# One start for every transfer: moving the data of every other SBUF slot by 128 bytes

## Chip, cores and metric

The kernel runs on one core of a Trainium2 chip. Its time is device time in microseconds, from one launch. Before the change three runs gave 1687.97, 1688.45 and 1688.55 us; their median is 1688.45 us.

The engines go by short names: PE (TensorE, matrix products and transposes), DVE (VectorE), ACT (ScalarE), POOL (GpSimd) and SP (SyncE, which here does nothing but issue transfers). HBM is the memory off the core, SBUF the one on it, with 128 partitions; PSUM takes what PE computes.

## What is computed

One decoding step of an attention block with a cache, followed by a gated feed-forward block, forwards and backwards. The results are the output and the gradients of eight inputs.

```python
def _A_ref(x, k_cache, v_cache, wq, wo):        # x: 4 x 1 x 512
    q = (x @ wq).reshape(B, 1, 32, 128).transpose(0, 2, 1, 3)
    scores = einsum("bhqd,bhkd->bhqk", q, k_cache) * (128 ** -0.5)
    p = softmax(scores)
    o = einsum("bhqk,bhkd->bhqd", p, v_cache)   # caches: 4 x 32 x 4096 x 128, bf16
    return o.transpose(0, 2, 1, 3).reshape(B, 1, 4096) @ wo
...
h = x + _A_ref(layernorm(x), k_cache, v_cache, wq, wo)
return h + swiglu(layernorm(h), w1, w3, w2)     # 512 -> 1792 -> 512
...
out, vjp = jax.vjp(f, x, k_cache, v_cache, wq, wo, w1, w3, w2)
return (out, *vjp(grad_out))
```

There are 4 x 32 = 128 heads. For each, K and V are 4096 x 128 in bf16, 1 MB. The gradients of the two caches, `out_2` and `out_3`, have the same size. So K is read once, V twice (forwards and backwards), and both gradients are written once: five times 134 MB, beside which the weights and their gradients are small.

## The kernel before

**The arena.** Nearly all SBUF data lives in one tile, `arena` (L112), of 23 slots. A slot is `SLOT` = 4160 elements of bf16 in each partition, 8,320 bytes. One head of K or V takes 4096 of them (32 rows of 128 in each partition), 8,192 bytes. The 4160 come from the tile `PK`, in which each of the 32 rows has two columns more (`PKW` = 130). In the built program the arena begins at byte 30,336 of each partition.

`Slot` (L125) takes one slot from the list `free` and makes a view of it, `self.t`; `b`, `f` and `heads` are views of that as bf16, as fp32 and as 32 rows of 128. `Slot2` (L146) takes two neighbouring slots that begin at an even number and views them as one piece, for two heads at once. `give` returns slots to the list. Which slot is taken depends on what was given back when, and not on addresses.

**The order of the work** is written out by hand (`tc.manual_schedule()`): each engine does its instructions in the order of the program text. All large transfers are issued by SP, on one queue; a transfer into a slot waits until the slot's last reader or writer is done.

**Forward** (L650 to L712): 64 groups of two heads. K and V of each head are loaded into slots (`load_K` L175, `load_V` L182; 1 MB each). K is transposed, a quarter by PE through PSUM (`T_pe` L352, copied back by ACT) and three quarters by DVE (`T_dve` L361). The scores (`S_head` L375) give the softmax; DVE multiplies K by the probabilities into a `PK` slot (`PK_mul` L455), PE multiplies V by that (`M_mm` L466), and ACT puts the 128 x 129 result of each head into an `M` slot (`M_end` L474, 16 heads in a slot, fp32). `PK` and `M` need more than 8,192 bytes of their slot.

**Middle** (L714 to L969): the output projection, the feed-forward block and the start of its backward pass. The weights are transposed here.

**Backward** (from L972): the first 32 heads one by one, the other 96 as 48 pairs of heads. V is loaded a second time (`load_V2` L836, 1 MB; `load_pair` L1292, 2 MB) and transposed in place by PE and ACT (`words_T` L793). The gradients of V and K are outer products that DVE writes into fresh slots (`outer` L812, `outer_pair` L1399), and SP stores them (`grad_V` L820, `grad_K` L1267, `grad_pair` L1407; 1 MB and 2 MB). The gradients of the weights go out in between (`side_work` L1017).

A transfer of a single head is 128 packets of 8,192 bytes, one for each partition, and one completion record on each of the 16 DMA engines. A pair of heads is 128 packets of 16,384 bytes.

Of the kernel before, what the change touches and what calls it, by code (L numbers as in the profile page):

```python
# [9 lines left out]
FP32 = mybir.dt.float32  # L10
# [7 lines left out]
SLOT = 4160  # L18
# [3 lines left out]
SP = 32  # L22
NPAIR = 8
OLD = 9


@with_exitstack
def kernel(
# [22 lines left out]
    nc = tc.nc  # L51
    P = nc.NUM_PARTITIONS

    B = A_x.shape[0]
    D = A_x.shape[-1]
    H = A_k_cache.shape[1]
    Sk = A_k_cache.shape[2]
    Dh = A_k_cache.shape[3]
    F = B_w1.shape[1]
    NH = B * H  # L60
# [4 lines left out]
    SJ = Sk // P  # L65
# [3 lines left out]
    PKW = Dh + 2  # L69
    MC = 16  # L70
# [41 lines left out]
    arena = slotp.tile([P, NSLOT * SLOT], BF16, name="arena")  # L112
# [12 lines left out]
    class Slot:  # L125
        def __init__(self, name, src=free):
            self.i = src[0]
            if part["B"] and src is free:
                lone = sorted((i for i in free if i not in part["pairs"]), key=age, reverse=True)
                self.i = lone[0] if name in SIDE or lone and age(lone[0]) >= OLD else max(free, key=age)  # L130
            src.remove(self.i)
            self.t = arena[:, self.i * SLOT:(self.i + 1) * SLOT]

        def b(self, n=4096):
            return self.t[:, 0:n]
# [10 lines left out]
    class Slot2:  # L146
# [5 lines left out]
        def __init__(self):  # L152
            self.i = min(self.choices())[1]
            free.remove(self.i)
            free.remove(self.i + 1)
            self.t = arena[:, self.i * SLOT:(self.i + 2) * SLOT]

        def give(self):
            gave(self.i, self.i + 1)
# [13 lines left out]
    Ks, Vs, KTs, PKs = {}, {}, {}, {}  # L173
# [34 lines left out]
    for i in range(2):  # L208
        t = fcon.tile([P, 64], BF16, name=f"onesw{i}")
# [4 lines left out]
    def ones_window(col):  # L214
# [11 lines left out]
                          in_=rowg[:, None, :, None].to_broadcast([P, 4, 8, 4]))  # L226
# [17 lines left out]
    OT_f = pers.tile([P, NH], FP32, name="OT_f")  # L244
# [80 lines left out]
    Ms = []  # L325

    def M_of(s):
        return Ms[s // MC].f(MC * (Dh + 1)).rearrange("p (n c) -> p n c", c=Dh + 1)[:, s % MC, :]

    c1 = ExitStack()  # L330
    c1b = ExitStack()
# [117 lines left out]

    def PK_pairs(s):  # L450
        PKs[s] = Slot("PK")
        PK = PKs[s].t[:].rearrange("p (j c) -> p j c", c=PKW)
        nc.gpsimd.tensor_copy(out=PK[:, :, Dh:PKW], in_=P_all[:, s, :, None].to_broadcast([P, SJ, 2]))  # L453

    def PK_mul(s):  # L455
        PK = PKs[s].t[:].rearrange("p (j c) -> p j c", c=PKW)
        nc.vector.tensor_tensor(  # L457
            out=PK[:, :, 0:Dh].rearrange("p j (r t) -> p j r t", t=2),
            in0=Ks[s].heads().rearrange("p j (r t) -> p j r t", t=2),
            in1=PK[:, :, None, Dh:PKW].to_broadcast([P, SJ, Dh // 2, 2]),  # L460
            op=ALU.mult,
        )
        Ks.pop(s).give()
        kdone["n"] += 1

    def M_mm(s, j0, j1):  # L466
        if j0 == 0:
            hold["M"] = psM.tile([P, PKW], FP32, name="M_ps", tag="M")
        PK = PKs[s].t[:].rearrange("p (j c) -> p j c", c=PKW)
        Vn = Vs[s].heads()  # L470
        for j in range(j0, j1):
            nc.tensor.matmul(hold["M"][:], lhsT=Vn[:, j, :], rhs=PK[:, j, :], start=(j == 0), stop=(j == SJ - 1))  # L472

    def M_end(s):  # L474
        w = s % 32
        PK = PKs[s].t[:].rearrange("p (j c) -> p j c", c=PKW)
        if w == 0:
            hold["kP"] = psK.tile([P, 4, Dh], FP32, name="kP_ps", tag="kP")
        for c in range(2):
            for q in range(4):  # L480
                j0 = (c * 4 + q) * 4
                nc.tensor.matmul(hold["kP"][32 * q:32 * (q + 1), :, :], lhsT=ones_window(w), rhs=PK[:, j0:j0 + 4, 0:Dh],  # L482
                                 start=(w == 0 and c == 0), stop=(w == 31 and c == 1), tile_position=(0, 32 * q))
        if s % MC == 0:
            Ms.append(Slot("M"))
        nc.scalar.copy(out=M_of(s), in_=hold["M"][:, 0:Dh + 1])
        PKs.pop(s).give()
        Vs.pop(s).give()
# [10 lines left out]


    def O_cols(s0, s1):
        nc.vector.tensor_copy(out=OT_f[:, s0:s1], in_=Ms[s0 // MC].f(MC * (Dh + 1)).rearrange("p (n c) -> p n c", c=Dh + 1)[
            :, s0 % MC:s0 % MC + s1 - s0, Dh])
        nc.vector.tensor_copy(out=OT_bf[:, s0:s1], in_=OT_f[:, s0:s1])

# [337 lines left out]
    with ExitStack() as cm:  # L843
# [70 lines left out]
        for sl in w1 + w3:  # L914
            sl.give()
        rs = Slot("reps")
# [1 line left out]
        part["pairs"] = {j for i in kept for j in (i, i + 1)}  # L918
        rep_bufs = {nm_: [rs.b()[:, (2 * k + i) * 512:(2 * k + i + 1) * 512].rearrange("p (i d) -> p i d", i=REP) for i in range(2)]
                    for k, nm_ in enumerate(("rq", "rdo"))}  # L920
        dh = rs.f(2080)[0:B, 1024:1024 + D]
        while len(free) > 1:
            load_V2()

# [47 lines left out]
    with ExitStack() as c2:  # L972
# [44 lines left out]
        def side_work():  # L1017
# [1 line left out]
            nc.tensor.transpose(pt[:], OT_bf[:], ident_b[:])  # L1019
            nc.scalar.copy(out=O_sb[:], in_=pt[:])  # L1020
            yield
            t = rs.f(2080)[:, 1536:1536 + NH]
            nc.vector.tensor_tensor(out=t, in0=c_rep[:], in1=kPT[:], op=ALU.mult)
            nc.vector.tensor_tensor(out=t, in0=dq_ps[:, 0:NH], in1=t, op=ALU.subtract)
            nc.vector.tensor_scalar(out=dqT_bf[:], in0=t, scalar1=scale, scalar2=None, op0=ALU.mult)
# [93 lines left out]
            for i in range(2):  # L1119
                st = Slot("gw2")  # L1120
                hw = hh_rows[:, i * 7 * P:(i + 1) * 7 * P].rearrange("b (p k) -> b k p", k=7)
                for k in range(7):
# [4 lines left out]
                                  in_=st.b(7 * D).rearrange("p (c j) -> p c j", c=7))  # L1127
# [4 lines left out]
            for (rows, out_ap) in ((dg_rows, out_6), (du_rows, out_7)):  # L1132
                for i in range(2):
                    st = Slot("gw13")
                    nw = hhat_bf[0:B, i * 2 * P:(i + 1) * 2 * P].rearrange("b (p k) -> b k p", k=2)
                    for k in range(2):
                        for (f0_, w_) in f_chunks:
# [5 lines left out]
                                      in_=st.b(2 * F).rearrange("p (c f) -> p c f", c=2))  # L1143
                    st.give()
            r1.give()
            for h0 in range(0, H, 8):
                st = Slot("gwo")
                ow = oflat.b(HD)[0:B, h0 * P:(h0 + 8) * P].rearrange("b (p k) -> b k p", k=8)
                for k in range(8):
# [4 lines left out]
                                  in_=st.b(8 * D).rearrange("p (k j) -> p k j", k=8))  # L1154
# [143 lines left out]
        def load_pairs(t):  # L1298
            while npv["next"] < NT and (npv["next"] <= t or len(V2s) + 2 * len(pV) < 6 and len(Slot2.choices()) > 1
                                          and -min(Slot2.choices())[0] >= OLD - 2):  # L1300
                load_pair()
# [197 lines left out]
        for t in range(NT):  # L1499
            s = SP + 2 * t  # L1500
# [46 lines left out]
```

## Time and profile before

The profiled execution spans 1686.6 us from its first to its last instruction, 1.8 us less than the median of the runs.

| | |
|---|---|
| median of 3 runs | 1688.45 us |
| span of the profiled execution | 1686.6 us |
| bytes moved | 707.21 MB (422.59 read from HBM, 282.34 written) |
| mean rate over the span | 419 GB/s |
| loads of K, forwards | 128 of 1024 KB, 15.4 us from issue to landing (median) |
| loads of V, single heads | 160 of 1024 KB, 15.6 us |
| loads of V, pairs | 48 of 2048 KB, 31.7 us |
| stores of gradients, single heads and weights | 72 of 1024 KB, 19.8 us |
| stores of gradients, pairs | 96 of 2048 KB, 27.4 us |

How to read it: a digit in a row of slices is the busy share of one fortieth of the span, in tenths. Busy shares of engines are averages over stages, so they say which engine can bound a stage and not that it does. A transfer's time from issue to landing contains its wait behind the transfers ahead of it on the same DMA engines: a single head's packets alone need about 2.5 us. Where the text speaks of a packet's duration, it is that of the trace's record of this packet; where it says where a transfer begins, the address comes from the built program.

### The profile page before, as it was taken

What the parts mean: (1) busy time and instruction counts of PE and PEld (TensorE: products, weight loads), DVE (VectorE), ACT (ScalarE), POOL (GpSimd) and SP (SyncE); (2) the same over time, 40 slices, a digit from 0 to 9 for tenths busy, and PEclk for the clock granted to TensorE, in tenths of its full rate; (3) what the DMA queues carried; (4) which work ended last, traced back from release to release, by engine and by line L of the source; (5) the groups of instructions that cost most, each with busy time, mean ns of one, the idle gap of its engine ahead of it and who ended that gap; (6) DMA issues with size and microseconds to landing.
All of it is one profiled execution on the core that took longest, in us unless ns stands there. A gap on an engine that the chain in (4) does not pass through costs nothing.

```text
span 1686.6 us, 33967 instructions
## 1 busy us (share of the span) xinstructions
PE 1260.6 (75%) x14188; PEld 924.3 (55%) x14188; DVE 1233.9 (73%) x1198; ACT 960.9 (57%) x1492; POOL 379.6 (23%) x663
## 2 busy tenths in 40 slices
PE   5989888888888888878878666667766677776660
PEld 4777777677667766745555544544434444444440
DVE  5999899989998997667766476576565656555673
ACT  3455454445445454677666556666655676666650
POOL 1221222222232222234541131111120101011020
PEclk9999999999999999799899778777678676567775
DMA  9999999999999999999999999999999999999996
GB/s 400 424 424 424 425 423 425 424 424 421 418 423 411 424 411 397 398 410 426 425 426 428 429 429 429 431 430 429 429 430 430 429 429 431 430 429 431 430 429 259
DMA packets 80986, 707.21 MB, mean 419 GB/s; under 512 B 8748, under 2 KB 12984, under 8 KB 15296
## 3 DMA queue, kind: packets, MB, share of 16 engines
q1 hardware_dynamic: 80416, 704.94, 99.2%
q8 instruction: 112, 1.84, 0.4%
q14 instruction: 42, 0.34, 0.0%
q0 software_dynamic: 416, 0.10, 0.0%
HBM read 422.59 MB, written 282.34 MB: 418 GB/s over the span
## 4 chain that ended last, share of the span: by engine, by line
DMA 35%; DVE 7%; ACT 5%; PE 5%; issue 3%; DVEq 0%; SPq 0%; POOL 0%; ACTq 0%
DMA out_dram<-arena 34%; DVE arena L1400 7%; ACT arena L799 5%; PE pt_tps L798 1%; PE dq_ps L1007 1%; PE dP_ps L1245 1%; DMA arena<-in_A_v_cache_dram 1%; PE pt_wo L610 0%; DVEq L1542 0%; PE rep_ps L1186 0%; DVE dPr L1342 0%; ACT dPr L1221 0%; PE dOT_ps L773 0%; PE dPT_ps L1228 0%; PE c_ps L784 0%
## 5 line engine op out<-in xcount | busy, mean ns | idle before, releaser
L799 ACT COPY arena<-pt_tps 128x1024 bf16<-128x1024 bf16 x512 | 491.7, 1023 | 249.0 <-PE pt_tps L798 247.3
L798 PE MATMUL pt_tps<-ident_f,arena 128*128 128x128 f32 x2048 | 410.7, 356 | 202.9 <-DMA arena<-in_A_v_cache_dram 125.6
L798 PEld LDWEIGHTS pt_tps<-ident_f,arena 128*128 128x128 f32 x2048 | 304.1, 182 | 349.3 <-issue 191.6
L1400 DVE TENSOR_TENSOR arena<-arena 128x8192 bf16<-128x8192 bf16 x48 | 212.5, 4427 | 197.9 <-DMA out_dram<-arena 192.5
L457 DVE TENSOR_TENSOR arena<-arena 128x4096 bf16<-128x4096 bf16 x128 | 292.4, 2285 | 24.0 <-POOL arena L453 24.0
L472 PE MATMUL M_ps<-arena 128*128 128x130 bf16 x4096 | 286.9, 223 | 30.0 <-DMA arena<-in_A_v_cache_dram 29.2
L472 PEld LDWEIGHTS <-arena 128*128 128x128 bf16 x4096 | 254.6, 99 | 49.6 <-DMA arena<-in_A_v_cache_dram 42.5
L1400 DVE TENSOR_TENSOR arena<-dS,arena 128x8192 bf16<-128x8192 bf16 x48 | 212.3, 4424 | 67.6 <-DMA out_dram<-arena 67.6
L364 DVE STREAM_TRANSPOSE arena<-arena 128x512 f32<-128x512 f32 (+1 forms) x321 | 250.6, 797 | 0.0
L359 ACT COPY arena<-pt_tps 128x1024 bf16<-128x1024 bf16 x128 | 129.4, 1012 | 180.4 <-PE pt_tps L358 149.6
L1397 POOL COPY arena<-arena 128x128 bf16<-128x128 bf16 x48 | 43.7, 912 | 432.7 <-ACT arena L1374 200.0
L370 POOL TENSOR_TENSOR W<-qrep,wmask 128x128 bf16<-128x128 bf16 x128 | 120.8, 944 | 85.4 <-PE S_ps L390 70.6
L453 POOL COPY arena<-P_all 128x64 bf16<-128x64 bf16 x128 | 32.7, 256 | 412.5 <-ACT P_all L447 409.5
L1308 POOL COPY arena<-arena 64x4 bf16<-64x4 bf16 x96 | 68.8, 717 | 136.3 <-PE dP_ps L1328 108.6
L1328 PE MATMUL dP_ps<-arena 128*32 128x512 bf16 x768 | 84.4, 471 | 8.4 <-ACT arena L799 8.3
L813 DVE TENSOR_TENSOR arena<-dS,arena 128x4096 bf16<-128x4096 bf16 x32 | 73.1, 2291 | 21.8 <-DMA out_dram<-arena 21.5
L447 ACT COPY P_all<-pt_P 32x64 bf16<-32x64 bf16 x256 | 52.1, 203 | 54.1 <-PE pt_P L443 51.8
L358 PE MATMUL pt_tps<-ident_b,arena 128*128 128x128 bf16 x1024 | 80.8, 224 | 0.0
L482 PE MATMUL kP_ps<-arena,onesw 128*32 128x512 bf16 x1024 | 79.4, 387 | 0.0
L813 DVE TENSOR_TENSOR arena<-P,arena 128x4096 bf16<-128x4096 bf16 x29 | 66.3, 2291 | 17.7 <-DMA out_dram<-arena 17.5
L422 ACT ACTIVATE E<-S_ps,nm 128x256 f32<-128x256 f32 x64 | 30.4, 474 | 82.7 <-DVE nm L419 82.6
L991 PE MATMUL gps<-arena 4*128 4x512 bf16 x110 | 47.3, 452 | 39.0 <-ACT arena L985 39.0
(246 smaller groups left out, 1494.7 us busy)
## 6 DMA issues: line engine op xcount, KB each, us to landing
out_dram<-arena SPq DMA_DIRECT2D x96, 2048.0 KB, 27.4
arena<-in_A_v_cache_dram SPq DMA_DIRECT2D x160, 1024.0 KB, 15.6
arena<-in_A_k_cache_dram SPq DMA_DIRECT2D x128, 1024.0 KB, 15.4
arena<-in_A_v_cache_dram SPq DMA_DIRECT2D x48, 2048.0 KB, 31.7
out_dram<-arena SPq DMA_DIRECT2D x72, 1024.0 KB, 19.8
arena<-in_A_wq_dram SPq DMA_DIRECT2D x8, 1024.0 KB, 14.3
arena<-in_B_w_dram SPq DMA_DIRECT2D x8, 896.0 KB, 15.0
out_dram<-arena SPq DMA_DIRECT2D x6, 896.0 KB, 27.6
```

The costliest lines, as they stand in the source:

```text
L358: nc.tensor.transpose(pt[:, i, :], Kn[:, c * GW + i, :], ident_b[:])
L359: nc.scalar.copy(out=KT[:, c * GW:(c + 1) * GW, :], in_=pt[:])
L364: nc.vector.transpose(out=KT[:, c * w_:(c + n) * w_], in_=Kn[:, c * w_:(c + n) * w_])
L370: nc.gpsimd.tensor_tensor(out=W[:, hl], in0=qrep[:, :, s:s + 1].to_broadcast([P, 4, 32]), in1=wmask[:, hl, None, :].to_broadcast([P, 4, 32 ...
L457: nc.vector.tensor_tensor(out=PK[:, :, 0:Dh].rearrange("p j (r t) -> p j r t", t=2), in0=Ks[s].heads().rearrange("p j (r t) -> p j r t", t=2),
L472: nc.tensor.matmul(hold["M"][:], lhsT=Vn[:, j, :], rhs=PK[:, j, :], start=(j == 0), stop=(j == SJ - 1))
L482: nc.tensor.matmul(hold["kP"][32 * q:32 * (q + 1), :, :], lhsT=ones_window(w), rhs=PK[:, j0:j0 + 4, 0:Dh], start=(w == 0 and c == 0), stop ...
L798: nc.tensor.transpose(ptw[:, jj, :], w[:, 4 * g + jj, :], ident_f[:])
L799: nc.scalar.copy(out=v.rearrange("p (j d) -> p j d", d=Dh)[:, g * GW:(g + 1) * GW, :], in_=pt[:])
L813: nc.vector.tensor_tensor(out=dst.rearrange("p j (r t) -> p j r t", t=2), in0=col2[:, :, None, :].to_broadcast([P, SJ, Dh // 2, 2]), in1=r ...
L1328: nc.tensor.matmul(rows["acc"][32 * c:32 * (c + 1), :], lhsT=zt[t % B][:, k, ZP - m:ZP - m + 32], rhs=words_of(v, 2 * c + u, k), start=(pl ...
L1400: nc.vector.tensor_tensor(out=dst.rearrange("p (j r t) -> p j r t", r=Dh // 2, t=2), in0=col2[:, :, None, :].to_broadcast([P, 2 * SJ, Dh / ...
```

## The change

Slots of even number, and pairs of slots, hold their data 64 elements (128 bytes) further on. `Slot` keeps the whole slot as `self.w`; its data view `self.t` has 4096 elements and begins at `LEAD` in even slots, at 0 in odd ones. `PK` and `M`, which need the whole slot and are part of no transfer, use `self.w`. A pair's view begins at `LEAD` and runs to the end of its second slot. Two views of the slot `rs` are taken from 2048 instead of 2080 fp32 elements, since `self.t` is shorter; the elements that they use are the same. No slot is chosen in another way, and the program text issues the same instructions in the same order.

```diff
--- before.py
+++ after.py
@@ -22,6 +22,7 @@
 SP = 32
 NPAIR = 8
 OLD = 9
+LEAD = 64
 
 
 @with_exitstack
@@ -129,7 +130,9 @@
                 lone = sorted((i for i in free if i not in part["pairs"]), key=age, reverse=True)
                 self.i = lone[0] if name in SIDE or lone and age(lone[0]) >= OLD else max(free, key=age)
             src.remove(self.i)
-            self.t = arena[:, self.i * SLOT:(self.i + 1) * SLOT]
+            self.w = arena[:, self.i * SLOT:(self.i + 1) * SLOT]
+            o = (self.i + 1) % 2 * LEAD
+            self.t = self.w[:, o:o + SJ * Dh]
 
         def b(self, n=4096):
             return self.t[:, 0:n]
@@ -153,7 +156,7 @@
             self.i = min(self.choices())[1]
             free.remove(self.i)
             free.remove(self.i + 1)
-            self.t = arena[:, self.i * SLOT:(self.i + 2) * SLOT]
+            self.t = arena[:, self.i * SLOT + LEAD:(self.i + 2) * SLOT]
 
         def give(self):
             gave(self.i, self.i + 1)
@@ -325,7 +328,7 @@
     Ms = []
 
     def M_of(s):
-        return Ms[s // MC].f(MC * (Dh + 1)).rearrange("p (n c) -> p n c", c=Dh + 1)[:, s % MC, :]
+        return Ms[s // MC].w[:].bitcast(FP32)[:, 0:MC * (Dh + 1)].rearrange("p (n c) -> p n c", c=Dh + 1)[:, s % MC, :]
 
     c1 = ExitStack()
     c1b = ExitStack()
@@ -449,11 +452,11 @@
 
     def PK_pairs(s):
         PKs[s] = Slot("PK")
-        PK = PKs[s].t[:].rearrange("p (j c) -> p j c", c=PKW)
+        PK = PKs[s].w[:].rearrange("p (j c) -> p j c", c=PKW)
         nc.gpsimd.tensor_copy(out=PK[:, :, Dh:PKW], in_=P_all[:, s, :, None].to_broadcast([P, SJ, 2]))
 
     def PK_mul(s):
-        PK = PKs[s].t[:].rearrange("p (j c) -> p j c", c=PKW)
+        PK = PKs[s].w[:].rearrange("p (j c) -> p j c", c=PKW)
         nc.vector.tensor_tensor(
             out=PK[:, :, 0:Dh].rearrange("p j (r t) -> p j r t", t=2),
             in0=Ks[s].heads().rearrange("p j (r t) -> p j r t", t=2),
@@ -466,14 +469,14 @@
     def M_mm(s, j0, j1):
         if j0 == 0:
             hold["M"] = psM.tile([P, PKW], FP32, name="M_ps", tag="M")
-        PK = PKs[s].t[:].rearrange("p (j c) -> p j c", c=PKW)
+        PK = PKs[s].w[:].rearrange("p (j c) -> p j c", c=PKW)
         Vn = Vs[s].heads()
         for j in range(j0, j1):
             nc.tensor.matmul(hold["M"][:], lhsT=Vn[:, j, :], rhs=PK[:, j, :], start=(j == 0), stop=(j == SJ - 1))
 
     def M_end(s):
         w = s % 32
-        PK = PKs[s].t[:].rearrange("p (j c) -> p j c", c=PKW)
+        PK = PKs[s].w[:].rearrange("p (j c) -> p j c", c=PKW)
         if w == 0:
             hold["kP"] = psK.tile([P, 4, Dh], FP32, name="kP_ps", tag="kP")
         for c in range(2):
@@ -499,7 +502,7 @@
 
 
     def O_cols(s0, s1):
-        nc.vector.tensor_copy(out=OT_f[:, s0:s1], in_=Ms[s0 // MC].f(MC * (Dh + 1)).rearrange("p (n c) -> p n c", c=Dh + 1)[
+        nc.vector.tensor_copy(out=OT_f[:, s0:s1], in_=Ms[s0 // MC].w[:].bitcast(FP32)[:, 0:MC * (Dh + 1)].rearrange("p (n c) -> p n c", c=Dh + 1)[
             :, s0 % MC:s0 % MC + s1 - s0, Dh])
         nc.vector.tensor_copy(out=OT_bf[:, s0:s1], in_=OT_f[:, s0:s1])
 
@@ -918,7 +921,7 @@
         part["pairs"] = {j for i in kept for j in (i, i + 1)}
         rep_bufs = {nm_: [rs.b()[:, (2 * k + i) * 512:(2 * k + i + 1) * 512].rearrange("p (i d) -> p i d", i=REP) for i in range(2)]
                     for k, nm_ in enumerate(("rq", "rdo"))}
-        dh = rs.f(2080)[0:B, 1024:1024 + D]
+        dh = rs.f(2048)[0:B, 1024:1024 + D]
         while len(free) > 1:
             load_V2()
 
@@ -1019,7 +1022,7 @@
             nc.tensor.transpose(pt[:], OT_bf[:], ident_b[:])
             nc.scalar.copy(out=O_sb[:], in_=pt[:])
             yield
-            t = rs.f(2080)[:, 1536:1536 + NH]
+            t = rs.f(2048)[:, 1536:1536 + NH]
             nc.vector.tensor_tensor(out=t, in0=c_rep[:], in1=kPT[:], op=ALU.mult)
             nc.vector.tensor_tensor(out=t, in0=dq_ps[:, 0:NH], in1=t, op=ALU.subtract)
             nc.vector.tensor_scalar(out=dqT_bf[:], in0=t, scalar1=scale, scalar2=None, op0=ALU.mult)
```

## The prediction

> **What bounds the kernel now.** I read the page's 40 slices first, then its queue line, then a table of stages, and last the costliest groups.
>
> ```profile
> span 1686.6 us, 33967 instructions
> ...
> PE 1260.6 (75%) x14188; PEld 924.3 (55%) x14188; DVE 1233.9 (73%) x1198; ACT 960.9 (57%) x1492; POOL 379.6 (23%) x663
> ...
> DMA  9999999999999999999999999999999999999996
> GB/s 400 424 424 424 425 423 425 424 424 421 418 423 411 424 411 397 398 410 426 425 426 428 429 429 429 431 430 429 429 430 430 429 429 431 430 429 431 430 429 259
> DMA packets 80986, 707.21 MB, mean 419 GB/s; under 512 B 8748, under 2 KB 12984, under 8 KB 15296
> ...
> q1 hardware_dynamic: 80416, 704.94, 99.2%
> ...
> DMA 35%; DVE 7%; ACT 5%; PE 5%; issue 3%; DVEq 0%; SPq 0%; POOL 0%; ACTq 0%
> ```
>
> No engine passes 75%, but the DMA row stands at 9 in every slice but the last, and SP's queue (q1) alone fills 99.2% of sixteen DMA engines' time. The chain of waits has DMA as its largest share, but follows only the last link at each step; the queue's own 99.2% is the better witness. So the time is the sum of the packets, and the change can act only through how long a packet takes or whether the queue runs dry.
>
> ```profile
> core 0: us, PE busy (x) PEld busy (x) DVE busy (x) ACT busy (x) POOL busy (x), PEclk, DMA share, GB/s
> ...
> 40.00:480.00 440.00, 380.33 (x6319) 311.74 (x6318) 406.59 (x542) 224.26 (x496) 110.44 (x264) 0.99 1.01 423
> ...
> 900.00:1620.00 720.00, 497.97 (x3100) 324.78 (x3100) 439.26 (x226) 463.17 (x573) 112.20 (x152) 0.74 1.01 430
> 1620.00:1687.00 67.00, 13.46 (x80) 8.24 (x79) 38.16 (x19) 11.77 (x13) 8.86 (x2) 0.60 0.75 319
> ```
>
> This is the table by stages; the last two columns are the share of the DMA engines' time and the rate. From 40 to 480 us only single heads are loaded; by the addresses worked out below, 53% of those bytes start 128 bytes off. From 900 to 1620 us nearly all is pairs of heads, and 98% of the bytes start off. The stage with nearly everything off moves more, 430 against 423 GB/s. Its packets are also twice as long, so this alone settles nothing, and I go to the packets.
>
> **The change, part by part.** The arena begins at byte 30,336 of each partition, which is 118.5 times 256; a slot is 8,320 bytes, 32.5 times 256. So an even slot, and every pair (it begins at an even slot), starts 128 bytes past a multiple of 256, an odd slot on one. Of SP's 530 transfers 361 start off (155 single loads of heads or wq/wo pages, 3 of weights, 48 pair loads, 53 single stores, 6 weight stores, 96 pair stores), 528 of 705 MB. Afterwards none does: even slots and pairs move up by LEAD, 64 elements or 128 bytes. The pattern does what its words say.
>
> 1. *Instructions, waits, queues.* The built programs have the same instructions with the same waits in the same order on all five engines. Nothing is added, removed or moved past anything: 0 us, and no cover is needed.
>
> 2. *A packet that starts off.* This is the whole question. The trace records each packet with size and duration. Of 47,104 packets of 8,192 bytes, 44,289 took 309 ns (94%); of 18,432 of 16,384 bytes, 17,428 took 611 ns (95%). The next packet of the same DMA engine begins 3 to 4 ns before the one ahead ends, so these durations are the throughput. A further 8,192 bytes cost 611 - 309 = 302 ns, so 128 bytes' worth of time is 302/64 = 4.72 ns. Single heads lie in both kinds of slot, so if starting off cost that, the 8,192-byte packets would fall into two groups of similar weight, 4.7 ns apart. There is one group.
>
> The same at the scale of a transfer: the 16 completion records of each transfer give a median time, and the difference to the transfer before is its interval. Behind another transfer of one slot, transfers of one slot that start on a multiple of 256 come 2,453 ns apart (median of 155), those that start off also 2,453 ns (median of 186). Eight packets at 309 - 3.3 ns and a 6 ns completion make 2,452; starting off at 4.7 ns a packet would have made 2,490. Loads alone and stores alone give 2,453 too. For pairs I have no aligned one to compare, but 4,862 ns (median of 144) is 8 x 607 + 6: exactly twice the bytes with the same small overhead per packet, so nothing is left to take away there. The value I take is 0 ns for each of the 361 transfers.
>
> 3. *Stretched packets.* 2,789 packets of 8,192 bytes took longer than 309 ns, in all 9.8 us of sixteen engines' time, and 1,004 of 16,384 bytes longer than 611, 1.7 us. The trace doesn't say what stretches them, and they are the one cost that an address could move. Bounds: all of them gone is -11.5 us, twice as many is +11.5 us. Between these I take 0: from 40 to 480 us, with half the bytes off, 6.0% of packets are stretched; from 900 to 1620 us, with 98% off, 4.8%. Regressing each forward transfer's stretch (cut at 60 ns) on its own alignment gives 3 ns more for one that starts off, of 17, over some 2,450 ns: under 1 us for all 208 that start off.
>
> 4. *Engine operands.* All that reads or writes a slot moves with its data, while the PK and M slots stay (they keep the whole slot). Whether 128 bytes matter to an engine, the same trace tells, since both kinds of slot occur.
>
> ```profile
> L457 DVE TENSOR_TENSOR arena<-arena 128x4096 bf16<-128x4096 bf16 x128 | 292.4, 2285 | 24.0 <-POOL arena L453 24.0
> ...
> L1400 DVE TENSOR_TENSOR arena<-arena 128x8192 bf16<-128x8192 bf16 x48 | 212.5, 4427 | 197.9 <-DMA out_dram<-arena 192.5
> ```
>
> These are two of the costliest groups: busy time and mean of one instruction, then idle time and its releaser. Split by whether the K slot and the PK slot begin on a multiple of 256, the 128 products of line 457 average 2,284, 2,284, 2,285 and 2,285 ns. The block transposes of line 364 have medians of 690 to 698 ns in the four combinations. So 0 here; were there some ns, DMA covers them, since line 1400 already waits 192.5 us for slots that stores free. Without that cover, 1 ns on each of the 14,188 matmuls would be 14 us, but no row shows it.
>
> 5. *Smaller views.* The reduced lengths, f(2080) to f(2048), address the same elements: 0.
>
> The sum is 0 against 1686.6 us of span. The runs' median lies 1.8 us above that, outside the profiled instructions; nothing there changes. Forecast: 1688.4 us.
>
> A rule of the Trainium skill speaks against this sum. "DMA: Bandwidth & Descriptors", section "How a descriptor splits into AXI transactions", says that a transaction must start at a multiple of 256 bytes, so that a descriptor starting later pays for the unused bytes before its start as well. The page does not say that it holds for SBUF addresses on both sides of a copy; this trace, with one duration for both kinds of slot, disagrees for these loads and stores.
>
> **The rivals.**
>
> *The bytes before the start are paid for (faster).* The number of packets that start off: 18,432 of 16,384 bytes, 208 x 128 = 26,624 of 8,192, and 1,408 of weights, 46,464 in all. At 4.72 ns over sixteen engines that is 13.7 us: 1674.8. For it: the queue is full, so every ns per packet would show. Against it: one duration, one interval. It would need a cost that the packet records hide although they fill the span. 6%. (This is the page's rule as a mechanism of this kernel.)
>
> *The stretch goes away (faster).* If off starts cause the stretched packets: up to 11.5 us, 1677.0. For it: they are more frequent from 40 to 480 us than later only by a point, so hardly anything; against it, the regression and the 98% stage. 4%.
>
> *Transfers fall in step (slower).* Now two kinds of start alternate in the queue; afterwards all packets on all sixteen DMA engines have one phase of the 256 bytes, and so do all heads that the engines read meanwhile. If like phases hinder each other in SBUF, more packets are stretched. The place is the forward stage, where phases are mixed today; twice the stretch is +11.5 us, 1699.9. It decides from 0.3 times that, 3.4 us, on. Against it: the pair stage has had one phase for 720 us, at 4.8% stretched against the forward stage's 6.0%. 8%.
>
> *It doesn't do what it says.* If the arena began on a multiple of 256, LEAD would put the even slots off. Byte 30,336 excludes that; and by part 2 the time would be the same.
>
> **How the numbers follow.** No change has 82%; 0.2% of 1688 us, 3.4 us, is about what a measurement of this kernel can tell from none. Faster takes 6% and 4%, slower 8%. The predicted time is that of the likeliest case. Its own range is 1685 to 1692. I lower the lower end to 1683, to take in about half of the stretch gone, and leave the upper end, since the pair stage speaks against the slower one; the far ends, 1674.8 and 1699.9, stay outside with less than 2 in 10.
>
> **What would show it.** Right: the 8,192-byte packets still at 309 ns and the 16,384-byte ones at 611, the stages at 423 and 430 GB/s, q1 at 99%, line 457 at 2,285 ns, and the chain ending in the same stores. Wrong towards faster: packets at 304 to 305 ns or at 606, and some 426 and 433 GB/s in the two stages. Wrong towards slower: the same 309 ns mode with more than 8% of packets above it, and the loss between 40 and 700 us. A loss with unchanged packets would have to be a dry queue, a 7 or 8 in the DMA row, and that would prove part 1 or 4 wrong.

## The result, and the profile after

| | median | lowest to highest | runs |
|---|---|---|---|
| before, on the same chip | 1688.89 us | 1687.97 to 1692.58 | 7 |
| after | 1684.34 us | 1683.10 to 1685.09 | 7 |

The ratio is 0.9972 [0.9961, 0.9983]: 4.5 us or 0.28% faster. That lies inside the forecast range, but on the side to which the prediction gave 10%: it is a small gain and not none. The prediction's own range ended at 1685 us; the result is inside only because the lower end was moved to 1683, to take in half of the stretched packets' time. The forecast said that the change costs and gains nothing, and that was wrong; that its range holds the number is luck. The profiled execution went from 1686.6 to 1681.3 us, 5.3 us less.

The page of the kernel after, with the lines that answer to those of before:

```profile
span 1681.3 us, 33967 instructions
...
DMA  9999999999999999999999999999999999999996
GB/s 400 425 425 424 425 424 425 425 425 423 418 425 410 424 414 403 411 411 425 426 426 428 429 430 430 430 429 431 429 429 431 428 430 429 431 429 430 431 430 277
DMA packets 80987, 707.21 MB, mean 421 GB/s; under 512 B 8749, under 2 KB 12985, under 8 KB 15297
...
q1 hardware_dynamic: 80416, 704.94, 99.4%
...
DMA 36%; DVE 8%; ACT 4%; PE 4%; issue 3%; DVEq 0%; SPq 0%; POOL 0%; ACTq 0%
...
L460 DVE TENSOR_TENSOR arena<-arena 128x4096 bf16<-128x4096 bf16 x128 | 292.5, 2285 | 22.8 <-POOL arena L456 21.7
L475 PE MATMUL M_ps<-arena 128*128 128x130 bf16 x4096 | 286.0, 222 | 13.1 <-DMA arena<-in_A_v_cache_dram 12.9
```

The instructions and their durations are those of before (line 457 is now 460, with 2,285 ns again), and the queue is as full as it was. The gain is spread thinly: most slices differ by 1 GB/s or not at all. The slices around 630 to 760 us (403, 411 and 411 in place of 397, 398 and 410) stand out, the middle stage with its weights, and so does the last slice (277 in place of 259), where the kernel ends. PE's idle time before the 4,096 products of line 475, a wait for V, fell to 13.1 us. On the page of before the same row reads:

```profile
L472 PE MATMUL M_ps<-arena 128*128 128x130 bf16 x4096 | 286.9, 223 | 30.0 <-DMA arena<-in_A_v_cache_dram 29.2
```

This row is a weak witness, though. In `forward_only`, a kernel of the experiments below in which all loads of the forward stage start on a multiple of 256, it stands above before:

```profile
L476 PE MATMUL M_ps<-arena 128*128 128x130 bf16 x4096 | 285.4, 222 | 31.2 <-DMA arena<-in_A_v_cache_dram 30.3
```

The stages, after (columns: window and its length in us, busy time of the engines, granted clock of PE, share of the DMA engines, rate):

```profile
core 0: us, PE busy (x) PEld busy (x) DVE busy (x) ACT busy (x) POOL busy (x), PEclk, DMA share, GB/s
40.00:480.00 440.00, 381.01 (x6320) 311.24 (x6312) 406.38 (x541) 224.44 (x494) 110.71 (x264) 0.99 1.01 424
...
900.00:1620.00 720.00, 500.21 (x3122) 325.16 (x3122) 442.76 (x229) 466.89 (x575) 113.45 (x153) 0.74 1.01 430
1620.00:1687.00 67.00, 9.40 (x52) 6.11 (x52) 32.63 (x14) 8.20 (x9) 4.43 (x1) 0.60 0.70 298
```

424 against 423 GB/s forwards, 430 against 430 in the pair stage: the page alone can't place 5 us.

**Where the time is seen.** The trace holds the time of one transfer in two forms. The packet records and the queue's completion records, which the prediction used, are one. The other is the semaphore: the trace holds 16 updates of it for each transfer (8,480 for the 530), as many as there are DMA engines, and each is read here as the arrival of one engine's part. The trace names no engine, so arrivals are put in order of time. The interval is the time of an arrival less that of the same rank in the transfer before; "on" starts at a multiple of 256 bytes, "off" does not. Forward loads 12 to 254, without two of w2 and the load behind them, median of all arrivals:

| | on after on | off after on | on after off | off after off | mean, all kinds |
|---|---|---|---|---|---|
| before | 2,437 ns (47 loads) | 2,472 (64) | 2,437 (64) | 2,477 (65) | 2,458.3 |
| after | 2,452 (240) | | | | 2,454.3 |

The mean leaves out intervals more than some 150 ns from the median; the plain means of all, which a few long gaps dominate, are 2,500.7 and 2,495.5 ns.

Before, a load that started off landed 35 to 40 ns later than one that started on, some 4.4 to 5 ns for each of the 8 packets that a DMA engine moves for it. The kinds were there side by side in the trace of before, while completion records gave both 2,453. The mean falls by only 4.0 ns, for a load that starts on makes up time when others lie between (2,437 against the 2,452 of a stream without any off). 240 x 4.0 is 1.0 us; measured at transfer 240, the median arrival is 1.2 us earlier (603.9 to 602.7 us). How far one execution can be trusted here, the experiments tell: in the four profiled kernels whose forward loads are those of before, transfer 240 is there at 603.5 to 603.9 us, in the three that have all of them on at 602.4 to 602.8.

The whole 5.3 us, followed along the 530 transfers: the median arrival gains 1.2 us up to transfer 240, 0.9 more by transfer 270 (wo pages and weights), 1.2 more by transfer 300 (the middle stage; in 700 to 720 us the granted clock was 0.91 in place of 0.83), and loses 0.3 from there to the last. That is 3.0. The other 2.3 us are the last arrival's: in both kernels one of the sixteen falls further and further behind the median in the pair stage, while the second last stays some 2 us behind, and it ends the kernel. It is read here as one DMA engine, the same throughout. At the last transfer it lagged 14.3 us before and 11.95 us after.

The packet records did change in two things. Packets of 8,192 bytes longer than 309 ns fell from 2,789 to 969 (from 40 to 480 us, from 6.0% to 0.6%), though the time above 309 ns fell only from 9.8 to 7.9 us of sixteen engines, and the usual 309 and 611 ns stayed; and of the 1,024-byte packets of the wo pages, 44% took over 46 ns before, 1% after.

### The profile page after: what moved, and what is told of

Its sections match the earlier page's. It is cut to its first block, busy times and chain, and to the rows that moved or that the text cites. A ratio compares the mean times of both kernels' runs of the same rounds, so it can differ in the third digit from the quotient of the medians.

```text
span 1681.3 us, 33967 instructions
## 1 busy us (share of the span) xinstructions
PE 1259.9 (75%) x14188; PEld 919.9 (55%) x14188; DVE 1233.6 (73%) x1198; ACT 961.0 (57%) x1492; POOL 380.8 (23%) x663
## 3 DMA queue, kind: packets, MB, share of 16 engines
q1 hardware_dynamic: 80416, 704.94, 99.4%
## 4 chain that ended last, share of the span: by engine, by line
DMA 36%; DVE 8%; ACT 4%; PE 4%; issue 3%; DVEq 0%; SPq 0%; POOL 0%; ACTq 0%
DMA out_dram<-arena 35%; DVE arena L1403 7%; ACT arena L802 4%; PE pt_tps L801 1%; PE dq_ps L1010 1%; DMA arena<-in_A_v_cache_dram 1%; PE dP_ps L1248 1%; PE pt_wo L613 0%; DVE arena L816 0%; DVEq L1545 0%; PE rep_ps L1189 0%; DVE dPr L1345 0%; PE dOT_ps L776 0%; ACT dPr L1224 0%; PE dPT_ps L1231 0%
## 5 line engine op out<-in xcount | busy, mean ns | idle before, releaser
L460 DVE TENSOR_TENSOR arena<-arena 128x4096 bf16<-128x4096 bf16 x128 | 292.5, 2285 | 22.8 <-POOL arena L456 21.7
L475 PE MATMUL M_ps<-arena 128*128 128x130 bf16 x4096 | 286.0, 222 | 13.1 <-DMA arena<-in_A_v_cache_dram 12.9
L475 PEld LDWEIGHTS <-arena 128*128 128x128 bf16 x4096 | 254.9, 100 | 31.2 <-DMA arena<-in_A_v_cache_dram 20.0
L1311 POOL COPY arena<-arena 64x4 bf16<-64x4 bf16 x96 | 64.5, 672 | 141.4 <-PE dP_ps L1331 114.1
L816 DVE TENSOR_TENSOR arena<-P,arena 128x4096 bf16<-128x4096 bf16 x29 | 66.3, 2291 | 17.6 <-DMA out_dram<-arena 16.9
## 6 DMA issues: line engine op xcount, KB each, us to landing
arena<-in_A_wq_dram SPq DMA_DIRECT2D x8, 1024.0 KB, 14.3
```

Of the source, the lines that this page charges most:

```text
L460: nc.vector.tensor_tensor(out=PK[:, :, 0:Dh].rearrange("p j (r t) -> p j r t", t=2), in0=Ks[s].heads().rearrange("p j (r t) -> p j r t", t=2),
L816: nc.vector.tensor_tensor(out=dst.rearrange("p j (r t) -> p j r t", t=2), in0=col2[:, :, None, :].to_broadcast([P, SJ, Dh // 2, 2]), in1=r ...
```

## The experiments

All are edits of the kernel after. Each ratio is that to the kernel before, measured on the same chip in the same series, with its 95% interval. No experiment leaves work out.

### Everything off, and one side at a time

`all_128` turns the change round: every transfer starts 128 bytes past a multiple.

```diff
-            o = (self.i + 1) % 2 * LEAD
+            o = self.i % 2 * LEAD
...
-            self.t = arena[:, self.i * SLOT + LEAD:(self.i + 2) * SLOT]
+            self.t = arena[:, self.i * SLOT:(self.i + 2) * SLOT]
```

> Every transfer starts 128 bytes past a multiple of 256 (odd slots moved up, even slots and pairs as before): 530 of 530 start off, against 361 before and 0 after. Theory A (each off start of a load costs by itself, by packets that are now and then stretched): the forward stage, where the changed kernel won 1.0 us by transfer 240 and 2.2 us by transfer 270 with 53% of the bytes put right, loses that share again for the other 47%: 1690 to 1692, and over 10% of the 8 KB packets between 40 and 480 us stretched. Theory B (only the mixture of two starts costs, since neighbouring packets differ): as fast as the changed kernel, 1684 to 1685, with under 1% stretched there. Theory C (the addresses of other things matter, not where a transfer starts): no order with the number of off starts.

Measured: 1696.01 us, 1.0044 [1.0032, 1.0057]. The stages:

```profile
core 0: us, PE busy (x) PEld busy (x) DVE busy (x) ACT busy (x) POOL busy (x), PEclk, DMA share, GB/s
40.00:480.00 440.00, 375.67 (x6250) 308.93 (x6249) 401.21 (x531) 221.48 (x490) 108.08 (x260) 0.99 1.01 419
900.00:1620.00 720.00, 504.17 (x3098) 326.99 (x3098) 439.86 (x226) 463.89 (x572) 109.82 (x150) 0.72 1.01 430
```

The forward stage, half off before, drops to 419 GB/s, and the pair stage, 98% off before, stays at 430. Forward arrivals come 2,484 ns apart (mean 2,484.8), 30.5 ns more than after; 240 x 30.5 is 7.3 us, measured 7.2 at transfer 240. Now the packet records show it too: 65% of the 8,192-byte packets from 40 to 480 us are stretched. Off starts cost time, and the cost per load is far larger when all are off than the 4 ns of the mixture of before.

`loads_only` leaves the gradients' stores as they were before, `stores_only` the loads. The first:

```diff
+OUT = ("gv", "gk", "gwq", "gw2", "gw13", "gwo")
...
-            o = (self.i + 1) % 2 * LEAD
+            o = (self.i + 1) % 2 * LEAD if name not in OUT else 0
...
-            pV[t] = Slot2()
+            pV[t] = Slot2(LEAD)
...
-            g_ = Slot2()
+            g_ = Slot2(0)
```

The second has `name in OUT`, `Slot2(0)` and `Slot2(LEAD)`. In both, data of one slot no longer begin at one place, and six copies of ACT get a further wait for an earlier transfer.

> Slots and pairs that are loaded hold their data as in the changed kernel, those that are stored from as before: 0 of 356 loads and 155 of 174 stores start off. Theory A says that loads alone paid (the pair stage, mostly stores and all off, kept its 430 GB/s): within 1 us of the changed kernel, 1684 to 1686. If stores pay as much as loads per byte (324 of the 528 MB that start off are stores), 1687. The lag of the slowest DMA engine in the pair stage (14.3 us before, 12.0 after) should go with whichever of the two pays.

> The mirror image: stores as in the changed kernel, loads as before (206 of 356 loads start off, no store). Theory A: as before, 1688 to 1689, with 6% of the 8 KB packets stretched between 40 and 480 us. If stores pay per byte like loads: 1686.

Measured: 1685.06 us, 0.998 [0.9971, 0.9989] for the loads, 1688.56 us, 1.0001 [0.9992, 1.001] for the stores, of which 155 of 174 start off in the one and none in the other. PE's wait for V is 23.3 us in `loads_only` and 40.7 in `stores_only`, but in kernels with the same forward loads as `loads_only` it lies between 13.1 and 31.2 us, so it does not decide. The times and the arrivals do: in `stores_only` the forward loads still come 2,472 to 2,478 ns after the one ahead if they start off and 2,433 to 2,437 if not, and transfer 240 is there at 603.5 us against 602.4 in `loads_only`. Stores show next to nothing: behind another store, single ones that start off have medians of 2,455 to 2,461 ns before, all on 2,453 after; pair stores 4,858 and 4,861. So it is the writing into SBUF that pays; for the stores, which read SBUF, no cost can be told from none at 128 bytes.

### A fixed price, a backlog, or the changes between kinds

Three accounts were left of why a mixture pays less: each off start costs the same (E in the expectations), a backlog builds up and only long runs of off loads pay (D), or each change between kinds costs (F). `runs_of_R` makes about half of all loads off in each case, singly or in runs of 16:

```diff
+    def off_next():
+        nth["load"] += 1
+        return (nth["load"] - 1) // RUN % 2 == 1
...
+            if name in LOADS and off_next():
+                o = LEAD - o
...
-            self.t = arena[:, self.i * SLOT + LEAD:(self.i + 2) * SLOT]
+            o = 0 if load and off_next() else LEAD
+            self.t = arena[:, self.i * SLOT + o:(self.i + 2) * SLOT]
```

`LOADS` are the names of slots that loads fill. Here, too, data of one slot begin at several places, and the built programs have further waits, nearly all for earlier transfers: on 91 instructions of ACT, DVE and POOL in `runs_of_1`, on 82 in `runs_of_16`.

> The changed kernel, but every second load in the order of the queue starts 128 bytes past a multiple of 256 (178 of 356 loads); all stores start on one. With all loads and stores off the time was 1696.0, with none 1684.3. Theory D (backlog: a packet that starts off leaves its DMA engine some ns behind; a buffer hides that, packets that start on a multiple let it catch up, and only a long enough run of off transfers overflows it): as the changed kernel, 1684 to 1685.5, with under 2% of the 8 KB packets between 40 and 480 us stretched. Theory E (each off start of a load has a fixed chance and cost, whatever stands beside it): half of the 11.7 us, 1690. Theory F (a change between the two starts costs): the slowest of all, above 1690.

> The same number of off loads (176 of 356), but 16 on a multiple and then 16 off, in turn. Theory D: the first two or three transfers of each off run are free and the others cost what they cost in the kernel with all at 128, so 40 to 45% of 11.7 us: 1689 to 1690, and some 25 to 30% of the packets between 40 and 480 us stretched, in bursts. Theory E: as with runs of one, 1690 in both. Theory F: as the changed kernel, since there are only 22 changes.

Measured: 1686.73 us, 0.999 [0.9981, 0.9999] with 178 of 356 loads off singly, and 1688.69 us, 1.0 [0.9991, 1.0008] with 176 in runs of 16. The stage of `runs_of_1`:

```profile
core 0: us, PE busy (x) PEld busy (x) DVE busy (x) ACT busy (x) POOL busy (x), PEclk, DMA share, GB/s
40.00:480.00 440.00, 382.70 (x6327) 312.24 (x6326) 407.21 (x542) 224.53 (x496) 109.32 (x264) 0.99 1.01 424
```

and of `runs_of_16`:

```profile
core 0: us, PE busy (x) PEld busy (x) DVE busy (x) ACT busy (x) POOL busy (x), PEclk, DMA share, GB/s
40.00:480.00 440.00, 380.15 (x6312) 311.24 (x6310) 405.42 (x539) 223.40 (x495) 110.00 (x264) 0.99 1.01 422
```

As many off loads make 424 or 422 GB/s, by their order. The slices on the page of `runs_of_16` let it be seen: 16 loads take about 39 us, a slice is 42 us, and the rates of slices 2 to 8 rise and fall.

```profile
GB/s 401 421 425 420 426 421 424 421 425 422 417 423 406 423 413 401 401 408 425 426 426 428 429 429 429 430 429 430 429 430 430 429 429 432 429 428 432 429 428 263
```

The stretched packets (310 to 330 ns) that begin between one landing and the next (of 128), by the place of the later transfer in a run of off loads, transfers 12 to 249; the 4th and 5th of before rest on five and three loads, the others on seven or more:

| | on | 1st | 2nd | 3rd | 4th | 5th | 6th | 7th | 11th |
|---|---|---|---|---|---|---|---|---|---|
| before | 3.5 | 1.8 | 8.2 | 17.3 | 53.2 | 40.7 | | | |
| runs_of_16 | | 0.4 | 3.0 | 6.6 | 8.2 | 10.4 | 33.8 | 60.8 | 80 |
| after | 0.3 | | | | | | | | |

A single off load stretches hardly anything; before from the fourth in a row on, and in `runs_of_16` from the sixth, a quarter of the packets and more are longer. The arrivals give the price. In `runs_of_1` off loads come 2,471 ns after the one ahead and the others 2,437, and the mean of 2,454.8 is nearly that of the kernel after (2,454.3): a single off load is all but made up for. At transfer 240 the kernel is 0.5 us behind the kernel after (603.3 and 602.7 us). Its whole time is 2.4 us above, with half of its pair loads off and the further waits; that rest is not placed. In `runs_of_16` off follows off at 2,483 ns and on follows on at 2,443, and the mean is 2,465.3. Over 240 loads the difference of 10.5 is 2.5 us; at transfer 240 it measures 2.1 (603.3 and 605.4 us). A fixed price would have made the two kernels equal, and one for changes would have made the single ones the dearer. The two ratios' intervals overlap a little, but the arrivals, 2.1 us apart where like kernels differ by 0.4, are against both. Of D the order is right and the sizes are off: it expected the single ones between 1684 and 1685.5 and the runs between 1689 and 1690 us.

### Which parts of the loads

Each kernel aligns one kind and leaves the rest as before: pair loads (`ON = ()`), wo pages, or the forward loads with wq.

```diff
+ON = ("wo",)
...
-            o = (self.i + 1) % 2 * LEAD
+            o = (self.i + 1) % 2 * LEAD if name in ON else 0
...
-        def __init__(self):
+        def __init__(self, o=0):
-            self.t = arena[:, self.i * SLOT + LEAD:(self.i + 2) * SLOT]
+            self.t = arena[:, self.i * SLOT + o:(self.i + 2) * SLOT]
```

`pair_loads_only` has `pV[t] = Slot2(LEAD)` as well.

> The kernel before, with the 48 pair loads alone put on a multiple of 256. Theory D now says: a load's writing side takes 8 packets x 4 to 5 ns more on each DMA engine when it starts off; fifteen engines make that up behind the stores between, but the slowest engine, which sets the end, is behind all through the pair stage and pays in full: 48 x 8 x 4.7 ns = 1.8 us. So its lag at the last transfer falls from 14.3 to 12.5 us, the median engine's time stays within 0.5 us of before, and the time is 1687. Rival: the lag is another matter, and stays between 13.8 and 14.8 us: 1688.9.

> The kernel before, with the four pages of wo alone on a multiple of 256. Their packets have 1,024 bytes, so each costs 4 to 5 ns of some 42, ten per cent, if an off start costs by the packet: the four transfers, 9.8 us from the one before them to the last in the kernel before (8.8 us in the changed one), go down by 1 us, and nothing else changes: 1687.9. Rival: the 1 us is the clock and the waits of the stage around them, and the four transfers keep 9.5 us or more.

> The kernel before, with the loads of wq, K and V of the forward stage alone on a multiple of 256. Theory D: on and off alternate there at random, on ones land 2,437 ns and off ones 2,475 ns behind the transfer before, 53% off, so 2,457 to 2,458 a transfer against 2,453 to 2,454 with all on: 240 transfers x 4 to 5 ns = 1.0 to 1.2 us by transfer 240, kept to the end: 1687.8. No gain at all (1688.9) would mean that what the forward stage wins is lost again at the stage after it.

| | time | ratio | its own place |
|---|---|---|---|
| `forward_only` | 1687.19 us | 0.9991 [0.9982, 1.0] | transfer 240 at 602.8 us, 603.9 before |
| `pair_loads_only` | 1687.40 us | 0.9993 [0.9984, 1.0002] | lag of the last DMA engine 13.6 us, 14.3 before |
| `wo_only` | 1688.03 us | 0.9995 [0.9986, 1.0004] | from the load ahead to the last of the four wo pages 10.78 us, 12.05 before |

None of these times by itself can be told from the kernel before; against before's 1688.79 the medians are 1.6, 1.4 and 0.8 us lower, 3.8 in all, of the 4.5 that the change gave. The places speak more clearly. The forward loads gain their 1.1 us as expected. For the four wo pages the kernels that have all of them on show 10.8 to 11.4 us by this measure and those that have all of them off 11.8 to 12.6; the page's table of transfers says it in one line (KB each, and median us from issue to landing), `wo_only`:

```profile
arena<-in_A_wo_dram SPq DMA_DIRECT2D x4, 1024.0 KB, 11.6
```

and before:

```profile
arena<-in_A_wo_dram SPq DMA_DIRECT2D x4, 1024.0 KB, 13.2
```

The pair loads were expected to take the lag down to 12.5 us and took it to 13.6, while `runs_of_1`, with half of its pair loads off, stands at 13.4 and `forward_only`, with all of them off, at 14.0. In `pair_loads_only` six copies of ACT have a further wait as well. The direction agrees; the size of this term stays open.

### Other distances

If the bytes between the multiple and the start were the price, 64 and 32 bytes would be cheaper than 128 and 224 dearer. A tile of that size ahead of the arena moves the arena, and with it the data of every transfer, by 64, 32 or 224 bytes:

```diff
+    slotp.tile([P, 32], BF16, name="pad")
```

This is `all_64`; `all_224` has 112 elements, and `all_32` has 8, for which the built program sets 32 bytes aside. `all_16` moves the view inside the arena:

```diff
-    arena = slotp.tile([P, NSLOT * SLOT], BF16, name="arena")
+    arena = slotp.tile([P, NSLOT * SLOT + 8], BF16, name="arena")[:, 8:]
```

> The changed kernel with the arena 64 bytes further on: all 530 transfers start 64 bytes past a multiple of 256. If an off start costs one more transaction whatever its distance (theory A1): as the kernel with all at 128. If it costs by the unused bytes before the start (theory A2): half of that loss, some 1 to 1.5 us less than that kernel, so 1687 to 1688 if that one takes 1690. Theory B: as the changed kernel, 1684 to 1685.

> The changed kernel with the arena 32 bytes further on: all 530 transfers start 32 bytes past a multiple of 256. 64 bytes off took 1698.6 and 128 off 1696.0, so a cost by the unused bytes before the start is already ruled out. If it is one more transaction, whatever the distance: 1696 to 1699. If the distance to the next multiple of 256 counts (224 bytes here, 192 and 128 there): 1699 to 1701. If 128 bytes is a boundary of its own: as 64, 1698 to 1699.

> The same with 16 bytes: the start is no longer on a multiple of 32. If nothing below 32 bytes matters: as with 32 bytes. If writing parts of 32 bytes at both ends of each packet costs more: clearly above it, and then at least the 4.7 ns of 128 bytes per packet again, 13 us.

> The changed kernel with the arena 224 bytes further on: all 530 transfers start 224 bytes past a multiple of 256, so a packet of 8,192 bytes begins with a piece of 32 bytes and ends with one of 224, the mirror image of the kernel with 32 bytes. Starts 128, 64 and 32 bytes past took 1696.0, 1698.6 and 1701.7 us, and the packets' loads landed 2,485, 2,489 and 2,497 ns apart. If the cost is the one further piece plus the size of the smaller piece's neglect, alike at both ends: as 32 bytes, 1700 to 1703. If a short last piece is what costs: below the kernel at 128, 1692 to 1696. If unused bytes before the start count (224 here): the slowest of the four, above 1703.

| start past a multiple of 256 | time | ratio to before | above the kernel after | median arrival of transfer 240 |
|---|---|---|---|---|
| 0 (after) | 1684.34 us | 0.9972 [0.9961, 0.9983] | | 602.7 us |
| 128 | 1696.01 us | 1.0044 [1.0032, 1.0057] | 11.7 us | 609.9 us |
| 64 | 1698.57 us | 1.006 [1.0047, 1.0074] | 14.2 us | 610.9 us |
| 32 | 1701.70 us | 1.0079 [1.0066, 1.0091] | 17.4 us | 613.6 us |
| 224 | 1702.12 us | 1.0079 [1.0065, 1.0093] | 17.8 us | 612.9 us |
| 16 | 1722.72 us | 1.0203 [1.0189, 1.0217] | 38.4 us | 615.1 us |

The forward stage of `all_32`:

```profile
core 0: us, PE busy (x) PEld busy (x) DVE busy (x) ACT busy (x) POOL busy (x), PEclk, DMA share, GB/s
40.00:480.00 440.00, 373.11 (x6220) 306.65 (x6221) 399.67 (x530) 221.25 (x490) 107.99 (x258) 0.99 1.01 417
```

and of `all_224`:

```profile
core 0: us, PE busy (x) PEld busy (x) DVE busy (x) ACT busy (x) POOL busy (x), PEclk, DMA share, GB/s
40.00:480.00 440.00, 376.62 (x6221) 309.00 (x6223) 400.15 (x530) 221.16 (x489) 107.77 (x258) 0.98 1.01 416
```

32 and 224 cost the same, 417 and 416 GB/s, though seven times as many bytes lie before the start. So those bytes don't set the price. What 32 and 224 share is the size of the smaller piece into which the boundaries cut a packet's two ends, and the price rises as that piece falls: 128, 64, 32, 16. They also share the largest power of two that divides the start, which for all five starts is the same number; no run tells the two readings apart (a start at 96 bytes would, with pieces of 96 and 160 and a power of 32). Why either would cost more, no run here shows. The 38 us of `all_16` aren't all of this kind:

```profile
core 0: us, PE busy (x) PEld busy (x) DVE busy (x) ACT busy (x) POOL busy (x), PEclk, DMA share, GB/s
40.00:480.00 440.00, 371.20 (x6196) 306.08 (x6193) 398.42 (x529) 220.44 (x485) 106.30 (x258) 0.99 1.01 415
700.00:720.00 20.00, 10.92 (x112) 8.54 (x109) 4.91 (x15) 6.47 (x8) 0.00 (x0) 0.50 0.46 187
720.00:740.00 20.00, 16.67 (x229) 13.42 (x229) 12.28 (x18) 10.20 (x14) 8.87 (x18) 0.67 0.66 263
```

Forwards it has 415 GB/s, little below `all_32`. But from 700 to 740 us, in the middle stage, the queue stood at 0.46 and 0.66, which is (1 - 0.46) x 20 + (1 - 0.66) x 20 = 17.6 us of DMA time not used. All four runs lie within 1.5 us, so this is no accident of one execution. It is the program's: PE's transposes of the weights at line 604, each group of which ACT or DVE copies back, take 28 us in place of 9, since PE waits for these copies. In `all_16`:

```profile
L604 PE MATMUL pt_w<-ident_b,arena x112: 268/314/314, 692.6 to 720.4; 128*128 128x128 bf16 x112
...
  ACT arena L257: 20.0, 16
  DVE arena L259: 7.7, 8
```

and in the kernel after (in both, idle time in us before the line, of PE and of its weight loads together, and how often, by what ended it):

```profile
L604 PE MATMUL pt_w<-ident_b,arena x112: 216/219/219, 678.8 to 687.3; 128*128 128x128 bf16 x112
...
  issue: 0.6, 2
  ACT arena L257: 0.3, 1
```

In the built program of `all_16` a dozen of these transposes' weight loads (PEld) and a dozen of the copies wait for a copy ahead of them for which they don't wait in the kernel after; `all_32` and the other shifted arenas have the waits of the kernel after. The granted clock was low as well (0.50 and 0.67), but `all_32` has the same 314 ns a transpose without the loss. From transfer 270 to 300 `all_16` takes 95.0 us and `all_32` 77.9, so some 17 of the 38 us are put down to these waits and not to the start of the transfers. Why a view that begins 16 bytes on has them stays open.

No version was faster than the kernel after.

## Why the prediction was wrong, step by step

**What bounds the kernel** held: q1 at 99.4%, the same instructions in the same order, the chain with the same largest share. With the queue full, the few ns of a load were worth their number in time, as the reading said.

**Step 1** (instructions, waits, queues: 0), **step 4** (engine operands: 0) and **step 5** (smaller views: 0) held. Line 460 still takes 2,285 ns; of all that moved, it is the loads that gave the gain.

**Step 2** (an off start costs 0 ns, "there is one group" and "one interval") is the step that failed. Its observations were right and still hold: 309 and 611 ns before and after, completion records 2,453 ns apart for both kinds. The failure was to take them for the landing. The arrivals of the semaphores in the same trace of before were 2,437 and 2,472 to 2,477 ns apart. Both sets of numbers are measured; that packet records time the reading side, and that the writing side runs behind them with room for a few loads, is an inference from them and from the stretched packets, which appear only well into a run of off loads. The rival "the bytes before the start are paid for" asked for just this, "a cost that the packet records hide although they fill the span", and got 6%; that it would be seen as packets of 304 or 305 ns was the same error in the list of what would show it.

The Trainium skill, "DMA: Bandwidth & Descriptors", section "How a descriptor splits into AXI transactions", was set aside in the prediction because of that step. For a load at 128 bytes it comes near: 4.4 to 5 ns a packet against the 4.72 worked out from packet durations. By its words 224 bytes should cost more than 32, and 32 less than 128; `all_224`, `all_32` and `all_128` measured 1702.1, 1701.7 and 1696.0 us. There the measurement decides.

**That rival's size** was 13.7 us and the gain was 4.5. Three of its terms were too large, by the runs. Stores, which were counted like loads, pay nothing that shows (`stores_only`: 1.0001 [0.9992, 1.001], which leaves room for 1.4 us at most). In a mixture the loads that start on catch up, so that the forward loads gave 1.1 us where 129 off loads at 35 to 40 ns would have made 4.5 to 5.2. And the 48 pair loads, at most one transfer in three of their stage, did not bring the median arrival forward and showed at most in the lag of one DMA engine. One term was too small: the four wo pages, counted as 128 packets each, go in packets of 1,024 bytes, and gave some 1 us at their place.

**Step 3** (stretched packets, 0 between bounds of 11.5 us) had the right bounds and the wrong reading. The stretch did go: 2,789 to 969 packets. But it was a sign of the backlog and not the whole cost: the packets of q1 over sixteen engines sum to 1673.9 us before and 1670.8 after, 3.1 of the 5.3. The regression of a load's stretch on its own alignment found 3 ns because the stretch depends on the loads ahead: 1.8 packets at the first off load and 53.2 at the fourth. And the 98% stage, which was the argument against, is one where two transfers of three are stores.

**The rival "transfers fall in step"** is refuted: the kernel after has one phase for all, and it is faster than the mixture of before and the fastest of the six kernels with one phase; the stretch fell.

**The account** of the 5.3 us: 1.2 for the forward loads and 0.9 for wo pages and weights are shown by single parts at their places. The 2.3 of the last arrival's lag are the change's in direction (12.0 to 13.6 us in the three kernels whose pair loads are all on, 14.0 to 15.0 in `before`, `stores_only`, `wo_only`, `forward_only` and `all_128`, where all are off); `loads_only`, with the same loads, lagged 13.0 us and not 11.95, so the size can be off by 1. The 1.2 us between transfers 270 and 300, where the granted clock differs between the two executions and `loads_only` shows none of it, and the 0.3 lost afterwards, are not put down to the change.

## What to carry to other kernels

Where a full queue of large loads bounds a kernel, begin the data of each load at a multiple of 256 bytes in SBUF; here it was worth 0.28% against a mixture, 0.7% against all starts at 128 bytes and 1% against all at 32, while stores that start 128 bytes off cost nothing that shows. When a cost is looked for in transfers, compare the arrivals at the semaphores by kind, and not the packet durations alone, which can be equal while the landings differ. And a mixture understates a cost that others can catch up: a kernel in which everything has the suspected property tells more than a regression over half of it. Before a shifted kernel is compared, compare the waits of its built program too: `all_16` lost some 17 us in a stage with waits of its own.

## What was not expected of the hardware

- The same loads are 2,453 ns apart in the completion records and 2,437 or 2,472 to 2,477 in the semaphores' arrivals.
- One arrival of sixteen, read as one DMA engine, fell 11.95 to 16.8 us behind the median in all kernels of this case, mostly in the pair stage (9.0 of 14.3 us from transfer 380 on, before), and it ends the kernel. Why it does is open.
- 32 and 224 bytes past a multiple cost the same (1701.7 and 1702.1 us).
- The mean duration of the packets that fetch instructions (q8) moved with the loads' starts: 987 ns before, 932 after, 1,029 in `all_128`.
